# Stores and preparations dealt out differently over the engine queues of a layer-norm, Fourier-mixing and gated-MLP kernel

## The chip, the cores and the metric

The kernel runs on one core of one Trainium2 chip. A core has five engines that take their own instruction streams in order and meet only through semaphores: TensorE (PE; its weight loads are a row of their own, PEld), VectorE (DVE), ScalarE (ACT), GpSimd (POOL) and SyncE (SP). The last two serve here almost only to start transfers. The metric is the device time of one execution in microseconds (us), as the median of several runs; lower is better.

## The reference

```python
xn = _layernorm(x, axis=-1)
a = jnp.einsum("bsd,ed->bse", xn, dft_hid_re)
b = jnp.einsum("bsd,ed->bse", xn, dft_hid_im)
y = jnp.einsum("ts,bse->bte", dft_seq_re, a) - jnp.einsum("ts,bse->bte", dft_seq_im, b)
g = jnp.einsum("bsd,df->bsf", xn, w_gate)
u = jnp.einsum("bsd,df->bsf", xn, w_up)
h = _gelu(g) * u
return x + y + jnp.einsum("bsf,fd->bsd", h, w_down)
```

x is 1 x 2048 x 512, the hidden width of the MLP is 1792, and everything is float32.

## The kernel before

**Products.** A float32 operand is split into a high part (a copy in TensorE's fp32r format) and a low part (the rest). One product is then three matmuls, high x high, high x low and low x high (`mm3`, L86). `split_hi` (L72) is an ACT copy, `split_lo` (L75) a DVE subtraction that needs the ACT copy first. Large products are done by a scheme of seven block products in place of eight (numbers 0 to 6), which needs sums and differences of blocks beforehand, on DVE.

**Stages, in the order of TensorE.** First the layer norm and transposes, with the hidden transform of the first eight row tiles done plainly. Then units 0 to 13: each multiplies one block of gate or up weights with the first half of the rows, applies GELU or the product, and in between runs small down products (`dn`) whose results go to a DRAM buffer `partial` by adding transfers. Then the hidden transform of the second half of the rows, by seven products of four tiles each (`spectral(1, k, i)`, output tiles `sa` and `sb` in PSUM, order `S_ORDER` = 0, 1, 4, 5, 6, 3, 2). Then units 14 to 27 on the second half of the rows. Last, four passes (c, g) = (1,0), (0,0), (1,1), (0,1) of 16 steps each for the sequence transform: a step loads a panel of the two sequence matrices (`pan`, 512 or 768 KB in two transfers), sums its blocks (`sums`, L653 to L656), splits it (`ps` high, `pl` low; the smaller second half in the passes with g = 0 is `ps1`) and adds products into the PSUM banks `m`. The banks of a pass are seeded with the earlier partial sums by ACT (`seed`, L775) and drained at its end.

**What sets the order.** Everything is written out by hand, in program order per engine: an engine executes its instructions in the order of the text, and a wait of one holds all behind it. Preparation for later products is written between the products, so the place in the text decides when DVE and ACT reach it.

**Around the second half's transform.** While product number p runs, `prepare(S_ORDER[p + 2], i)` is called behind each of its four tiles: parts 0 and 2 are the block sums of x and of the weights (`sum_x` L308 to L314, `sum_w` L321 to L329), parts 1 and 3 their splits (`xT4h`, `w1h` and so on). ACT also copies PSUM tiles: `sb<-sa` after product 0 (L243), `a<-sa` after product 1 (L246). All eight PSUM banks are in use, four `sa` and four `sb`, so product 4 gets its first bank when the first `a<-sa` has been copied out. Behind the tiles of the first product stand also the four leftovers of unit 13 (`carry`): `hh`, `hl`, a product with `q`, and a second `hl`.

**Around pass one.** `background(27)` lists the work that the last unit spreads between its own products by cost: sums, split and side tiles (`a`, `s34`) of step 0, then weight splits (`wl<-wd`, `wl<-ws`), then sums and side tiles of step 1. The split of step 1's panel is written behind that, in step 0 (`prepare_step`).

**Around the last passes' ends.** `drain` handles the banks of a pass with g = 1 in the order r = 5, 4, 3, 1, with j = 0, 1: ACT copies bank 5 to `u`, DVE adds bank 4 to give `v` and bank 3 to give the second `u`, which is stored; bank 1 is copied to `o` and stored. `drain_rest` subtracts `v` from four further tiles `x` (L808) and stores them. After the third pass it is called in step 0 of the last pass; after the last pass behind bank 3. All stores but the two halves of the very last tile go through POOL (`store`, L800); those halves, copied by ACT and DVE (L837), go out by the queues of ACT and SP (L838).

Of the kernel before, what the change touches and what calls it, by code (L numbers as in the profile page):

```python
# [24 lines left out]
HD = D // 2  # L25
# [10 lines left out]
def fnet_geglu_kernel(ctx: ExitStack, tc: tile.TileContext, x, xt, cs, dh, wgu, wd, out):  # L36
# [4 lines left out]
    nc = tc.nc  # L41
# [35 lines left out]
    def split(t, src):  # L77
        split_hi(t, src)
        split_lo(t, src)
# [261 lines left out]
                w1[k, j_] = [v[:, j_] for v in w]  # L341
        return w1[k, j], wraw[{0: 0, 1: 1, 3: 3}[k], j] if k in (0, 1, 3) else wsum[k, j]

    def prepare(k, part):
        j = part // 2
        if part % 2 == 0:
            sum_x(k, j)
            sum_w(k, j)
        else:
            split(*x1_split(k, j))  # L350
            split(*w1_split(k, j))

# [104 lines left out]
    items, carry = [], []  # L459
# [18 lines left out]
    def background(n):  # L478
        work = []
        if n == 2 * NP - 1:  # L480
            work = [(None, lambda f=f: advance(f, 0), c) for f, c in ((sum_step, 2), (split_step, 6), (side_split, 3))]

        def put(f, *args, cost=2):
            work.append((None, lambda: f(*args), cost))

        def splits(f, *args, cost=2, then=lambda: None):
            t = []

            def begin():
                t.append(f(*args))  # L490
                split_hi(*t[0])
            work.append((begin, lambda: (split_lo(*t[0]), then()), cost))

        if n % 2 == 0 and n:
            for k in range(4):
                put(h_sum, n // 2 - 1, k)
        if 0 < n < 2 * NP - 1:
            for k in range(4):
                splits(weight_split, n + 1, k, cost=2 if k < 3 else 1)
        if n % 2 == 0 and n:  # L500
            for k in range(4):
                splits(h_split, n // 2 - 1, (2, 1, 0, 3)[k])
        if n % 2 == 0:
            for f in weight_sums(("d", n // 2)):
                put(f, cost=1)
        else:
            for k in range(4) if n < 2 * NP - 1 else (0, 2):
                splits(weight_split, ("d", n // 2), k, cost=2 if k < 3 else 1)
        if n + 2 < 2 * NP:
            for f in weight_sums(n + 2):  # L510
                put(f, cost=1)
        if n in (NP - 2, NP - 1):
            for j in range(2):
                splits(x1_split, n - NP + 2, j)
                splits(w1_split, n - NP + 2, j)
        for k in SIDE_AT.get(n, ()):
            for f in side_sums(k):
                put(f, cost=1)
        if n == 2 * NP - 1:
            put(advance, sum_step, 1)  # L520
            put(advance, side_split, 1, cost=3)
        if 4 <= n < 12:
            t, k = divmod(n - 4, 4)
            put(norm_xr, k // 2, t, k % 2, cost=4)
        return work
# [101 lines left out]
    tokens = {0: list(range(NS)), 1: [0, 1, 2, 3, 4, 12, 5, 13, 6, 14, 7, 15, 8, 9, 10, 11]}  # L627
    steps = [(c, g, n) for c, g in passes for n in tokens[g]]
    pan, pan_hl = {}, {}
    reached = {}  # L630

    def advance(f, upto):
        for k in range(reached.get(f, 0), upto + 1):
            f(k)
        reached[f] = max(upto + 1, reached.get(f, 0))
# [26 lines left out]
    def prepare_step(i):  # L662
        advance(sum_step, i)
        later = sums(i + 1) if reached[sum_step] == i + 1 else []
        reached[sum_step] = max(reached[sum_step], i + 2)
        if reached.get(split_step, 0) <= i < len(steps):
            reached[split_step] = i + 1
            low = [split_begin(i, k) for k in range(2)]
            del pan[i]
            if len(later) < 2:  # L670
                low[0]()
                low.pop(0)
        else:
            low = []
        for k in range(max(len(low), len(later))):
            for f in later[k:k + 1] + low[k:k + 1]:
                f()

    def split_begin(i, k):
        g = steps[i][1]  # L680
        two = g or k == 0
        t = (pair("ps"), pair("pl")) if two else hl_tile("ps1")
        src = pan[i][k]
        split_hi(t, src)
        for h, r in enumerate((((0, 6), (2,)), ((4, 5), (3, 1)))[g][k]):
            pan_hl[i, r] = [v[:, h] for v in t] if two else t
        return lambda: split_lo(t, src)

    def split_step(i):
        if i < len(steps):  # L690
# [106 lines left out]
        nc.gpsimd.dma_start(kept[c, k, j], t)  # L797

    def store(c, h, t, j, src):
        nc.gpsimd.dma_start(out[2 * h + j, 2 * c + t], src)  # L800

    us, vs = {}, {}

    def drain_rest(c):
        for j in range(2):
            for h in range(2):
                t = rest.pop((c, h, j))
                nc.vector.tensor_sub(t, t, vs[j])  # L808
                store(c, h, 1, j, t)

    def drain(c, r, j):
        ps = bank.pop((c, r, j))
        if r in (0, 6):
            t = ship("tot")
            nc.scalar.activation(t, ps, AF.Copy)
            if r == 6:
                keep(c, 0, j, t)
            for u in (5, 1) if r == 0 else (3,):
                nc.gpsimd.dma_start(partial[c, u, j], t, accum_op=OP.add)
        elif r == 2:  # L820
            t = ship("x2")
            nc.vector.tensor_sub(t, rest.pop((c, j)), ps)
            keep(c, 1, j, t)
        elif r == 5:
            us[j] = ship("u")
            nc.scalar.activation(us[j], ps, AF.Copy)
        elif r == 4:
            vs[j] = slot("v")
            nc.vector.tensor_add(vs[j], ps, us[j])
        elif r == 3:  # L830
            nc.vector.tensor_add(us[j], ps, us[j])
            store(c, 1, 0, j, us[j])
        elif (c, j) == (passes[-1][0], 1):
            t = ship("o")
            for (e, f), queue in zip(((nc.scalar.copy, slice(HD)), (nc.vector.tensor_copy, slice(HD, CH))),
                                     (nc.scalar, nc.sync)):
                e(t[:, f], ps[:, f])  # L837
                queue.dma_start(out[j, 2 * c, :, f], t[:, f])  # L838
        else:
            t = ship("o")  # L840
            nc.scalar.activation(t, ps, AF.Copy)
            store(c, 0, 0, j, t)
# [126 lines left out]
        unit(n)  # L969
    xT.clear()  # L970
    xT.update(xT_next)
    for p, k in enumerate(S_ORDER):
        for i in range(TPC):
            spectral(1, k, i)
            if p == 0:
                carry.pop(0)()
            if p + 2 < len(S_ORDER):
                prepare(S_ORDER[p + 2], i)
        xT.update(xT_next)
        if p == 4:  # L980
            load_wd(NP // 2)
# [9 lines left out]
    for i, (c, g, n) in enumerate(steps):  # L991
# [13 lines left out]
        elif at < NS - 1:  # L1005
            for k in range(i + 1, ahead + 1):
                prepare_step(k)
        if at == 0 and p == 3:
            drain_rest(passes[2][0])
        if p == 0:  # L1010
            advance(side_split, at + 2)
            while carry:
# [12 lines left out]
        for r in GROUP[g]:  # L1025
# [9 lines left out]
            if r == 3 and g and at == NS - 1:  # L1035
                if turn:
                    low()
                    del pan[i + 1]
                else:
                    drain_rest(c)  # L1040
            if items and r == 0 and at:
                (items.pop(0)() or (lambda: None))()
        if at == NS - 1:
# [39 lines left out]
```

## Time and profile before

| what | value |
|---|---|
| median of 3 runs | 813.76 us (813.72 to 814.07) |
| the profiled execution's own time | 813.86 us |
| its span, first to last instruction | 812.1 us |
| between the two | 1.8 us |
| DVE, ACT, POOL busy, share of the span | 85%, 62%, 22% |
| transfers | 190.02 MB, mean 234 GB/s |

The page lists busy time by engine; a matmul takes 389 ns from start to end but the next begins while it runs, so what counts on TensorE is the distance between starts. In a row of the timeline the columns are start, duration, engine, line, operation, output and inputs, shapes and count, and in square brackets the idle time of the engine just before and what ended it. In the list of waits they are who waited for whom, then the time in all, the number of times and the longest.

### The profile page before, as it was taken

What the parts mean: (1) busy time and instruction counts of PE and PEld (TensorE: products, weight loads), DVE (VectorE), ACT (ScalarE), POOL (GpSimd) and SP (SyncE); (2) the same over time, 40 slices, a digit from 0 to 9 for tenths busy, and PEclk for the clock granted to TensorE, in tenths of its full rate; (3) what the DMA queues carried; (4) which work ended last, traced back from release to release, by engine and by line L of the source; (5) the groups of instructions that cost most, each with busy time, mean ns of one, the idle gap of its engine ahead of it and who ended that gap; (6) DMA issues with size and microseconds to landing.
All of it is one profiled execution on the core that took longest, in us unless ns stands there. A gap on an engine that the chain in (4) does not pass through costs nothing.

```text
span 812.1 us, 11223 instructions
## 1 busy us (share of the span) xinstructions
PE 800.0 (99%) x3514; PEld 654.3 (81%) x3514; DVE 689.2 (85%) x1210; ACT 500.7 (62%) x880; POOL 178.6 (22%) x271
## 2 busy tenths in 40 slices
PE   8999999999999999999999999999999999999996
PEld 4887887888887888888888878888888888888885
DVE  6778999889899769999889988866898889889982
ACT  5667876675686566676676674755575654365531
POOL 2210212222221322343233230221202411020001
PEclk9999999999999999999999999999999999999999
DMA  9833546967993568988888997998999998589612
GB/s 339 308 105 112 200 118 144 216 123 174 236 234 96 191 141 191 280 265 208 213 192 206 251 272 246 323 345 251 323 396 397 278 404 340 198 279 369 240 52 103
DMA packets 80603, 190.02 MB, mean 234 GB/s; under 512 B 10192, under 2 KB 12768, under 8 KB 80416
## 3 DMA queue, kind: packets, MB, share of 16 engines
q1 hardware_dynamic: 53168, 119.57, 42.7%
q0 software_dynamic: 27088, 69.49, 34.6%
q8 instruction: 27, 0.44, 0.2%
q10 hardware_dynamic: 288, 0.26, 0.1%
q14 instruction: 32, 0.26, 0.1%
HBM read 133.17 MB, written 58.20 MB: 236 GB/s over the span
## 4 chain that ended last, share of the span: by engine, by line
PE 68%; issue 17%; DVE 6%; DMA 3%; ACT 3%; POOL 2%; POOLq 0%; SPq 0%; DVEq 0%; ACTq 0%
PE m L86 18%; PE dn L86 13%; PE b L86 12%; PE a L86 8%; PE c L86 8%; PE xp L86 5%; PE sb L86 2%; DMA qr<-sd 2%; PE sa L86 1%; POOL out_y L800 1%; DMA ar<-ab 1%; DVE ws L370 1%; DVE wl L75 1%; DVE s L431 1%; DVE hl L75 1%
## 5 line engine op out<-in xcount | busy, mean ns | idle before, releaser
L72 ACT ACTIVATE ps<-pan 128x1024 fp32r<-128x1024 f32 x96 | 100.5, 1059 | 93.2 <-PE m L86 48.7
L75 DVE TENSOR_TENSOR pl<-pan,ps 128x1024 fp32r<-128x1024 f32 x96 | 117.8, 1227 | 25.9 <-ACT ps L72 18.3
L456 POOL DMA_DIRECT2D partial<-part x86 | 75.8, 894 | 184.0 <-ACT part L452 172.1
L452 ACT ACTIVATE part<-dn 128x512 f32<-128x512 f32 x106 | 62.5, 601 | 29.5 <-PE dn L86 28.3
L75 DVE TENSOR_TENSOR wl<-ws,wh 128x512 fp32r<-128x512 f32 x84 | 55.3, 686 | 0.0
L86 PE MATMUL m<-ps,bth 128*128 128x512 f32 x128 | 49.8, 389 | 0.0
L86 PE MATMUL m<-pl,bth 128*128 128x512 f32 x128 | 49.8, 389 | 0.0
L86 PE MATMUL m<-ps,btl 128*128 128x512 f32 x128 | 49.8, 389 | 0.0
L72 ACT ACTIVATE wh<-ws 128x512 fp32r<-128x512 f32 x84 | 49.7, 628 | 0.0
L86 PE MATMUL m<-ps,a 128*128 128x512 f32 x128 | 44.7, 390 | 0.0
L593 ACT ACTIVATE w<-b 128x512 f32<-128x512 f32 x28 | 16.7, 597 | 39.1 <-PE b L86 39.0
L596 DVE TENSOR_TENSOR w<-c,w 128x512 f32<-128x512 f32 x28 | 19.4, 691 | 24.8 <-ACT w L593 24.6
L86 PE MATMUL b<-xT3h,w 128*128 128x512 f32 x112 | 39.1, 390 | 0.0
L75 DVE TENSOR_TENSOR htl<-s,hth 128x512 fp32r<-128x512 f32 x56 | 36.0, 689 | 2.9 <-ACT hth L72 2.9
L431 DVE TENSOR_TENSOR s<-s 128x512 f32<-128x512 f32 x56 | 37.4, 688 | 0.9
L86 PE MATMUL m<-ps,qrh 128*128 128x512 f32 x96 | 37.3, 389 | 0.0
L86 PE MATMUL m<-pl,qrh 128*128 128x512 f32 x96 | 37.3, 389 | 0.0
L86 PE MATMUL m<-ps,qrl 128*128 128x512 f32 x96 | 37.3, 389 | 0.0
L72 ACT ACTIVATE hh<-s 128x512 fp32r<-128x512 f32 x42 | 26.5, 635 | 10.7 <-PE dn L86 4.1
L72 ACT ACTIVATE hth<-s 128x512 fp32r<-128x512 f32 x56 | 32.4, 640 | 0.6 <-PE dn L86 0.6
L86 PE MATMUL dn<-hth,wh 128*128 128x512 f32 x80 | 31.1, 389 | 0.0
L86 PE MATMUL dn<-hth,wl 128*128 128x512 f32 x80 | 31.1, 389 | 0.0
(329 smaller groups left out, 2452.3 us busy)
## 6 DMA issues: line engine op xcount, KB each, us to landing
pan<-in_cs SPq DMA_DIRECT2D x96, 512.0 KB, 6.6
partial<-part POOLq DMA_DIRECT2D x106, 256.0 KB, 4.9
wx<-in_wgu SPq DMA_DIRECT2D x56, 256.0 KB, 4.4
abr<-ab SPq DMA_DIRECT2D x32, 256.0 KB, 6.5
pan<-in_cs SPq DMA_DIRECT2D x32, 256.0 KB, 6.5
wd<-in_wd SPq DMA_DIRECT2D x28, 256.0 KB, 4.4
old<-partial POOLq DMA_DIRECT2D x28, 256.0 KB, 6.4
b<-ab SPq DMA_DIRECT2D x20, 256.0 KB, 6.6
```

What stands on the lines that cost most here:

```text
L72: nc.scalar.activation(t[0], src, AF.Copy)
L75: nc.vector.tensor_sub(t[1], src, t[0].bitcast(F32))
L86: nc.tensor.matmul(ps, a[u][:, sl], b[v], start=first and r == 0, stop=last and r == 2, skip_group_check=resumed)
L370: nc.vector.tensor_tensor(r[k][:, h], u, v, op=op)
L431: nc.vector.tensor_sub(t, u, v)
L452: nc.scalar.activation(t, ps[j], AF.Copy)
L456: nc.gpsimd.dma_start(partial[sp, r, j], t, accum_op=OP.add)
L593: nc.scalar.activation(w, b, AF.Copy)
L596: nc.vector.tensor_add(w, c, w)
L800: nc.gpsimd.dma_start(out[2 * h + j, 2 * c + t], src)
```

## The change

Four things move; no arithmetic is added or removed, except that the last tile's two halves get a buffer each.

1. In the second half's transform, `prepare(k)` returns five pieces (sums of half 0; split of x half 0 and sums of half 1; split of the weights half 0; split of x half 1; split of the weights half 1). They go into a list `behind`, one is taken behind each tile, and two behind the first tile of every product but the first. The leftovers of unit 13 move from the first product's four tiles to the second tile of products 5, 6, 3 and 2.
2. In `background(27)` the sums of step 1 come directly behind the side tiles of step 0, and a new piece `begin_early(1, 0)` splits the first part of step 1's panel within the unit, ahead of step 1's side tiles.
3. The four subtractions and stores left from the third pass run two by two in steps 1 and 2 of the last pass in place of four in step 0. In the last pass two of them follow each `v`.
4. Stores of the last pass are issued by SyncE in place of POOL.

```diff
-    def prepare(k, part):
-        j = part // 2
-        if part % 2 == 0:
+    def prepare(k):
+
+        def sums(j):
             sum_x(k, j)
             sum_w(k, j)
-        else:
-            split(*x1_split(k, j))
-            split(*w1_split(k, j))
+
+        return (lambda: sums(0),
+                lambda: (split(*x1_split(k, 0)), sums(1)),
+                lambda: split(*w1_split(k, 0)),
+                lambda: split(*x1_split(k, 1)),
+                lambda: split(*w1_split(k, 1)))
...
-            work = [(None, lambda f=f: advance(f, 0), c) for f, c in ((sum_step, 2), (split_step, 6), (side_split, 3))]
+            work = [(None, lambda f=f, k=k: advance(f, k), c)
+                    for f, k, c in ((sum_step, 0, 2), (split_step, 0, 6), (side_split, 0, 3), (sum_step, 1, 2))]
...
-            put(advance, sum_step, 1)
+            put(begin_early, 1, 0, cost=1)
             put(advance, side_split, 1, cost=3)
...
-            low = [split_begin(i, k) for k in range(2)]
+            low = [early.pop((i, k), None) or split_begin(i, k) for k in range(2)]
...
+    def begin_early(i, k):
+        split_begin(i, k)()
+        early[i, k] = lambda: None
...
-        nc.gpsimd.dma_start(out[2 * h + j, 2 * c + t], src)
+        (nc.sync if c == passes[-1][0] else nc.gpsimd).dma_start(out[2 * h + j, 2 * c + t], src)
...
-    def drain_rest(c):
-        for j in range(2):
-            for h in range(2):
-                t = rest.pop((c, h, j))
-                nc.vector.tensor_sub(t, t, vs[j])
-                store(c, h, 1, j, t)
+    def drain_rest(c, j):
+        for h in range(2):
+            t = rest.pop((c, h, j))
+            nc.vector.tensor_sub(t, t, vs[j])
+            store(c, h, 1, j, t)
...
             nc.vector.tensor_add(vs[j], ps, us[j])
+            if c == passes[-1][0]:
+                drain_rest(c, j)
...
-            t = ship("o")
...
-                e(t[:, f], ps[:, f])
-                queue.dma_start(out[j, 2 * c, :, f], t[:, f])
+                t = ship("o")
+                e(t[:, :HD], ps[:, f])
+                queue.dma_start(out[j, 2 * c, :, f], t[:, :HD])
...
+    behind = []
     for p, k in enumerate(S_ORDER):
+        if p + 2 < len(S_ORDER):
+            behind.extend(prepare(S_ORDER[p + 2]))
         for i in range(TPC):
             spectral(1, k, i)
-            if p == 0:
+            if p > 2 and i == 1 and carry:
                 carry.pop(0)()
-            if p + 2 < len(S_ORDER):
-                prepare(S_ORDER[p + 2], i)
+            for f in behind[:2 if p and i == 0 else 1]:
+                f()
+            del behind[:2 if p and i == 0 else 1]
...
-        if at == 0 and p == 3:
-            drain_rest(passes[2][0])
+        if at in (1, 2) and p == 3:
+            drain_rest(passes[2][0], at - 1)
...
-                else:
-                    drain_rest(c)
```

The order of TensorE's instructions is the same in both programs. **ACT in the second half's transform, first two products, before:**

```order
L243 ACTIVATE sb<-sa 128x512
L72 ACTIVATE hh<-s 128x512
L243 ACTIVATE sb<-sa 128x512
L72 ACTIVATE xT4h<-xraw 128x512
L72 ACTIVATE w1h<-w1s 128x512
L243 ACTIVATE sb<-sa 128x512 x2
L72 ACTIVATE xT4h<-xraw 128x512
L72 ACTIVATE w1h<-w1s 128x512
L246 ACTIVATE a<-sa 128x512 x2
L72 ACTIVATE xT5h<-xraw 128x512
L72 ACTIVATE w1h<-w1s 128x512
L246 ACTIVATE a<-sa 128x512 x2
```

and with the change:

```order
L243 ACTIVATE sb<-sa 128x512 x2
L72 ACTIVATE xT4h<-xraw 128x512
L243 ACTIVATE sb<-sa 128x512
L72 ACTIVATE w1h<-w1s 128x512
L243 ACTIVATE sb<-sa 128x512
L72 ACTIVATE xT4h<-xraw 128x512
L246 ACTIVATE a<-sa 128x512
L72 ACTIVATE w1h<-w1s 128x512
L246 ACTIVATE a<-sa 128x512
L72 ACTIVATE xT5h<-xraw 128x512
L246 ACTIVATE a<-sa 128x512
```

Splits and PSUM copies now alternate, and the leftover `hh` is gone from here. **DVE at the same place, before:**

```order
L308 TENSOR_TENSOR xraw<-xraw 128x512
L321 TENSOR_TENSOR w1s<-d_2678,d_2716 128x512
L75 TENSOR_TENSOR hl<-s,hh 128x512
L75 TENSOR_TENSOR xT4l<-xraw,xT4h 128x512
L75 TENSOR_TENSOR w1l<-w1s,w1h 128x512
L417 SCALAR_TENSOR_TENSOR s<-s,q_2652 128x512
L308 TENSOR_TENSOR xraw<-xraw 128x512
L321 TENSOR_TENSOR w1s<-d_2681,d_2719 128x512
L75 TENSOR_TENSOR hl<-s,hh 128x512
L75 TENSOR_TENSOR xT4l<-xraw,xT4h 128x512
L75 TENSOR_TENSOR w1l<-w1s,w1h 128x512
```

and with the change:

```order
L308 TENSOR_TENSOR xraw<-xraw 128x512
L321 TENSOR_TENSOR w1s<-d_2678,d_2716 128x512
L75 TENSOR_TENSOR xT4l<-xraw,xT4h 128x512
L308 TENSOR_TENSOR xraw<-xraw 128x512
L321 TENSOR_TENSOR w1s<-d_2681,d_2719 128x512
L75 TENSOR_TENSOR w1l<-w1s,w1h 128x512
L75 TENSOR_TENSOR xT4l<-xraw,xT4h 128x512
L75 TENSOR_TENSOR w1l<-w1s,w1h 128x512
```

The second pair of sums stands three instructions earlier (one subtraction of the split and two leftovers are no longer ahead of it). **DVE at the end of unit 27, before pass one, before:**

```order
L417 SCALAR_TENSOR_TENSOR s<-s,w 128x512
L75 TENSOR_TENSOR wl<-wd,wh 128x512
L75 TENSOR_TENSOR wl<-ws,wh 128x512
L419 TENSOR_TENSOR s<-s,b 128x512
L75 TENSOR_TENSOR hl<-s,hh 128x512
L617 TENSOR_TENSOR q_5263<-c,q_5263 128x512
L653 TENSOR_TENSOR pan<-pan,pan_5074 128x512
L75 TENSOR_TENSOR a_5381<-ar,a_5381 128x256
L75 TENSOR_TENSOR s34l<-w_5078,s34h 128x512
L75 TENSOR_TENSOR pl<-pan,ps 128x1024
```

and with the change:

```order
L420 SCALAR_TENSOR_TENSOR s<-s,w 128x512
L657 TENSOR_TENSOR pan<-pan,pan_5074 128x512
L75 TENSOR_TENSOR wl<-wd,wh 128x512
L422 TENSOR_TENSOR s<-s,b 128x512
L75 TENSOR_TENSOR hl<-s,hh 128x512
L621 TENSOR_TENSOR q_5263<-c,q_5263 128x512
L75 TENSOR_TENSOR wl<-ws,wh 128x512
L75 TENSOR_TENSOR pl<-pan,ps 128x1024
L75 TENSOR_TENSOR a_5385<-ar,a_5385 128x256
L75 TENSOR_TENSOR s34l<-w_5078,s34h 128x512
```

Step 1's sum (`pan`) stands five instructions earlier and its low part `pl` two earlier, ahead of the side tiles. On ACT the high part `ps` changes places in the same way with `a` and `s34h` of step 1, and `wh<-ws` now stands between the first two and the last two seeds `m<-old`. **DVE at the end of the program, before:**

```order
L829 TENSOR_TENSOR v<-m,u 128x512 x2
L831 TENSOR_TENSOR u<-m,u 128x512 x2
L808 TENSOR_TENSOR x_7950<-x_7950,v 128x512
L808 TENSOR_TENSOR x_7951<-x_7951,v 128x512
L808 TENSOR_TENSOR x_7956<-x_7956,v 128x512
L808 TENSOR_TENSOR x_7957<-x_7957,v 128x512
L837 COPY o<-m 128x256
```

and SP's last stores with the change, which follow DVE's new order (two `x` behind each `v`, then both `u`):

```order
L808 DMA out_y<-x_7950 128x512
L808 DMA out_y<-x_7951 128x512
L808 DMA out_y<-x_7956 128x512
L808 DMA out_y<-x_7957 128x512
L808 DMA out_y<-u 128x512 x2
L808 DMA out_y<-o 128x512
L847 DMA out_y<-o 128x256
```

Before, SP had only the last of these rows, and POOL had the other seven in the order `u` twice, four `x`, `o`.

More of the change, by code (lines that the diff above doesn't have):

```diff
@@ L629, in fnet_geglu_kernel @@
     pan, pan_hl = {}, {}
-    reached = {}
+    reached, early = {}, {}
     def advance(f, upto):
```

## The prediction

> **What bounds the kernel now.** I read the page's busy times first, then every distance between starts of matmuls, then the waits of the weight loads, and last the timeline around the places found.
>
> ```profile
> PE 800.0 (99%) x3514; PEld 654.3 (81%) x3514; DVE 689.2 (85%) x1210; ACT 500.7 (62%) x880; POOL 178.6 (22%) x271
> ```
>
> TensorE sets the time, and the change leaves its instructions and their order as they are. So a gain can come from two sources only: from stalls of TensorE that the busy share hides, and from what follows the last matmul. The first stall, in the second half's transform (TensorE's timeline):
>
> ```profile
> 250.75 0.39 PE L86 MATMUL sa<-w1h,xT1l 128*128 128x512 f32 x1
> 250.98 0.39 PE L86 MATMUL sa<-w1h,xT1h 128*128 128x512 f32 x1
> 251.21 0.39 PE L86 MATMUL sa<-w1l,xT1h 128*128 128x512 f32 x1
> 251.43 0.39 PE L86 MATMUL sa<-w1h,xT1l 128*128 128x512 f32 x1
> 252.42 0.50 PE L86 MATMUL sa<-w1h,xT4h 128*128 128x512 f32 x1 [0.60 <-ACT a L246]
> 252.75 0.39 PE L86 MATMUL sa<-w1l,xT4h 128*128 128x512 f32 x1
> ```
>
> Undisturbed starts lie (251.43 - 250.75) / 3 = 0.227 us apart. The step to 252.42 is 0.99, and the next one 0.33: a stop costs its wait and about 0.11 more. The stage as a whole begins and unit 14 begins with
>
> ```profile
> 240.54 0.39 PE L86 MATMUL sa<-w1h,xT0h 128*128 128x512 f32 x1
> ```
> ```profile
> 280.09 0.39 PE L86 MATMUL a<-xT0h,wh 128*128 128x512 f32 x1
> ```
>
> That is 39.55 us for 7 products x 4 tiles x 6 = 168 matmuls, which at 0.2267 take 38.09: **1.46 us are lost here**. The waits of the weight loads in this stretch name PSUM copies on ACT as releasers, `a` for two stops (below) and `sb` for a third and smaller one, ahead of them:
>
> ```profile
> PEld sa L86 <- ACT a L246: 1.4, 2, 1.0
> ```
>
> The second place is the start of pass one, in step 1:
>
> ```profile
> 484.32 0.40 PE L86 MATMUL m<-ps,a 128*128 128x512 f32 x1
> 485.38 0.50 PE L86 MATMUL m<-pl,a 128*128 128x512 f32 x1 [0.66 <-DVE pl L75]
> ```
>
> The third is step 2 of the last pass:
>
> ```profile
> 728.73 0.39 PE L86 MATMUL m<-ps,qrb 128*128 128x512 f32 x1
> 729.39 0.50 PE L86 MATMUL m<-pl,qrb 128*128 128x512 f32 x1 [0.27 <-DVE pl L75]
> ```
>
> They cost 1.06 - 0.23 + 0.11 = 0.94 and 0.66 - 0.23 + 0.11 = **0.54 us**, and both times TensorE waits for DVE's low part. The last place is the end. Landings there (the list of transfers; the last figure is us from issue to landing), then the late issues (timeline), and the transfer engines (a table by stretches; its last two columns are their busy share and GB/s):
>
> ```profile
> out_y<-u POOLq DMA_DIRECT2D x2, 256.0 KB, 2.3
> out_y<-o POOLq DMA_DIRECT2D x1, 256.0 KB, 3.8
> out_y<-o ACTq DMA_DIRECT2D x1, 128.0 KB, 2.4
> out_y<-o SPq DMA_DIRECT2D x1, 128.0 KB, 3.1
> ```
>
> ```profile
> 806.06 0.35 ACTq L838 DMA_DIRECT2D out_y<-o  x1
> 806.06 0.42 DVE L837 COPY o<-m 128x256 f32<-128x256 f32 x1
> 806.51 0.34 SPq L838 DMA_DIRECT2D out_y<-o  x1
> 807.13 0.54 POOL L800 DMA_DIRECT2D out_y<-o  x1
> ```
> ```profile
> 805.00:810.50 5.50, 0.62 (x3) 0.19 (x1) 1.46 (x3) 0.37 (x1) 2.36 (x5) 0.96 0.92 334
> ```
>
> The last transfer to be issued is not of the last tile: it is the `o` of j = 0, held in POOL's queue behind four `x`. It lands at 807.13 + 3.8 = 810.93, and the end of the span at 812.06 is 1.13 later. The engines are nearly full until 810.5.
>
> **The change, part by part. First, the second half's transform.** The chain behind the late PSUM copies, on ACT:
>
> ```profile
> 247.03 0.63 ACT L72 ACTIVATE xT4h<-xraw 128x512 fp32r<-128x512 f32 x1 [2.43 <-DVE xraw L308]
> ```
> ```profile
> 250.64 0.63 ACT L72 ACTIVATE xT4h<-xraw 128x512 fp32r<-128x512 f32 x1 [1.41 <-DVE xraw L308]
> 251.25 0.63 ACT L72 ACTIVATE w1h<-w1s 128x512 fp32r<-128x512 f32 x1
> 251.78 1.06 ACT L246 ACTIVATE a<-sa 128x512 f32<-128x512 f32 x2
> ```
>
> and the sum that the second of these splits waits for, on DVE:
>
> ```profile
> 249.92 0.69 DVE L308 TENSOR_TENSOR xraw<-xraw 128x512 f32<-128x512 f32 x1
> ```
>
> ACT stands idle with `xT4h` at the head of its queue, waiting for a sum on DVE, while two PSUM copies whose products are done stand behind it. DVE starts an instruction of this size every 0.60 us (727.51 to 728.12 in the rows of the third part). Three instructions leave the way of the second sum, so it starts at about 248.3 in place of 249.92 (three times 0.60, less some 0.2 in which DVE now waits for the first `xT4h`, done at 247.66). ACT's second `xT4h` then starts near 249.05, and the first `a<-sa` stands directly behind it: 249.05 + 0.53 (ACT's distance, 251.25 to 251.78) = 249.6, landing by 250.2. TensorE wants that bank at 251.4 less what it gained before. Margin: over 1 us. The `sb` copies come at 247.6 and 248.6 by the same count, before TensorE's 248.7 and 250.1. The third `a` waits behind `xT5h`, whose sum follows four more DVE instructions: near 252.6, wanted at 254.1. So all three stops go. The leftovers return behind products 5 to 2: one `hl` of them before the last split of product 2. From the first sum (started near 246.3, as it released ACT at 247.03) to that split the new order has 41 DVE instructions, 24.7 us at 0.60 each, so it is done near 271 plus DVE's own waits. TensorE wants it near 274.1: the stage's new end, 278.6, less four tiles of 1.36, plus four matmuls. Some 3 us are left for waits. Value: **-1.4 us**. Bounds: -1.46 if every loss goes, -0.7 if the copies of the third bank or a late split stop it once more.
>
> **Second, pass one.** ACT ahead of the late split, then DVE:
>
> ```profile
> 482.05 0.42 ACT L72 ACTIVATE a<-ar 128x256 fp32r<-128x256 f32 x1
> 482.36 0.63 ACT L72 ACTIVATE s34h<-w 128x512 fp32r<-128x512 f32 x1
> 483.00 1.06 ACT L72 ACTIVATE ps<-pan 128x1024 fp32r<-128x1024 f32 x1
> ```
> ```profile
> 484.10 1.23 DVE L75 TENSOR_TENSOR pl<-pan,ps 128x1024 fp32r<-128x1024 f32 x1 [0.19 <-ACT ps L72]
> ```
>
> DVE's `pl` starts as soon as `ps` is done, so moving the panel's sum forward on DVE is not what pays. `ps` gets rid of `a` and `s34h` ahead of it (482.05 to 483.00, 0.95 us) but takes on `wh<-ws` (0.53), which stood before the seeds and is now between them. It starts 0.42 earlier, and `pl` with it. TensorE resumes at about 484.97 in place of 485.38. The low part of `a`, now behind `pl`, is ready at about 485.26, just when TensorE comes to it at 485.3. The later seeds come 0.5 us later, near 481.6, when TensorE comes to them; a short stop there would only use up some of the wait that follows. Value: **-0.4 us**. Bounds: -0.1 (the side tile late too) and -0.94 (the whole stop).
>
> **Third, the last pass, steps 1 and 2:**
>
> ```profile
> 725.11 2.50 DVE L808 TENSOR_TENSOR x<-x,v 128x512 f32<-128x512 f32 x4
> 727.51 0.69 DVE L654 TENSOR_TENSOR pan<-pan 128x512 f32<-128x512 f32 x1
> 728.12 1.22 DVE L75 TENSOR_TENSOR pl<-pan,ps 128x1024 fp32r<-128x1024 f32 x1
> ```
>
> With the four `x` out of the way, that `pl` runs from 725.7 to 726.95, 2 us before TensorE asks at 728.96. Two `x` then stand in each of the next two steps (1.25 us each), where by the same count `pl` for step 3 ends near 732.3, wanted at 734.5. Value: **-0.54 us**, bounds -0.3 and -0.54. This and the first gain shift everything behind them alike, since transfers and splits there wait for TensorE to free buffers.
>
> **Fourth, the end.**
>
> ```profile
> 798.93 0.69 DVE L829 TENSOR_TENSOR v<-m,u 128x512 f32<-128x512 f32 x1 [9.89 <-PE m L86]
> ```
>
> The first `x` can be stored at 798.93 + 0.69 + 0.62 (a quarter of the four `x` above) = 800.25. Today the first store waits for a `u`, which by the order comes behind both `v`. Eight such instructions end by about 803.9. Seven stores of 0.262 MB at 334 GB/s take 0.78 us each: 800.25 + 2.3 (a landing on quiet engines, `u`) + 6 x 0.78 = 807.3. So the engines are drained when the halves come. DVE's copy may still follow ACT's (a separate buffer frees it of one tie; the built program keeps a wait on ACT). So SP issues between 806.1, as ACT does now, and 806.5, as SP does now; I take 806.5. A half lands 2.3 to 3.1 later; I take ACT's 2.4, being the nearest. 806.5 + 2.4 + 1.13 = 810.0 in place of 812.06: **-2.0 us**. Bounds: 806.1 + 2.3 + 1.13 gives -2.5, 806.5 + 3.1 + 1.13 gives -1.3.
>
> Sum: 1.4 + 0.4 + 0.54 + 2.0 = 4.34. The profiled execution took 813.86 with a span of 812.06, so 809.5; the median lies 0.1 under it, so **809.4 us**.
>
> **The rivals.** *The end is bound by the transfer engines, not by a queue.* For it: 334 GB/s and a share of 0.92 up to 810.5. Then SP only saves the difference of the last issues, 807.13 - 806.51 = 0.6, and the time is 813.76 - 2.34 - 0.6 = 810.8. Against it: the first store now stands before both `u`, not behind them. The Trainium skill has this rule ("DMA: Bandwidth & Descriptors", section "Issuing engines are not separate DMA queues"): transfers of all queues run on the same 16 engines, and a second issuing engine saves only the time to issue. By that rule the move to SP alone is worth those 0.6 us; the rest of my 2.0 hangs on DVE's order.
>
> *The transform's stop moves instead of going*: the leftovers and the four subtractions behind product 6 crowd DVE, and its own waits for ACT eat the 3 us and 1.2 more before product 2 is split. That gives back 1.2: 810.6. For it: the wait of 1.41 us above shows that ACT and DVE hold each other up. Against it: before, with two leftovers more, product 2 came without a stop.
>
> *DVE becomes the bound in the last pass.* For it:
>
> ```profile
> 740.00:780.00 40.00, 40.00 (x178) 33.14 (x177) 40.00 (x52) 21.11 (x23) 0.00 (x0) 1.00 0.68 243
> 780.00:800.00 20.00, 20.00 (x90) 16.55 (x89) 9.68 (x12) 5.45 (x6) 0.00 (x0) 1.00 0.00 0
> ```
>
> DVE (third pair) is full for 40 us. If TensorE, earlier by the gains of pass one and of steps 1 and 2, caught up with it, those 0.94 would be lost: 810.3. Against it: DVE is done half way through the next 20 us, so it works ahead.
>
> *Better:* the whole stop of pass one goes and the end takes its far bound: 808.4.
>
> *It doesn't do what it says:* the stops return one instruction on, and a half on SP lands behind seven stores as late as POOL's last does, 806.51 + 3.8 + 1.13 = 811.44, so 0.6 is left: 813.1.
>
> *Slower:* SP's queue stops in the transform. The leftovers now hold their buffers to product 2, and as built the load of `wd` waits for TensorE too.
>
> ```profile
> 256.88 2.89 SPq L400 DMA_DIRECT2D wd<-in_wd  x2
> ```
> ```profile
> 295.93 0.42 DVE L370 TENSOR_TENSOR ws<-wd 128x256 f32<-128x256 f32 x1
> ```
>
> Behind it stand unit 16's weights. It decides from 291.5 on, when a landing of 4.4 us (`wd` in the page's list of issues) misses 295.93; to come out slower it must be held to 296. At 300 the loss is 8.5 and the time 817.9. Against it: the leftovers end near 277.
>
> **How the numbers follow.** Forecast 0.62, better 0.08, end by the transfer engines 0.10, transform 0.08, DVE 0.04, not as it says 0.05, slower 0.03. The forecast's own bounds run from 808.6 (1.46 + 0.6 + 0.54 + 2.5) to 811.0 (-1.3 - 0.1 - 0.3 - 1.1), which also takes in three of the rivals. About 0.2% (1.6 us) is what a measurement can tell from no change: faster 0.92, same 0.05, slower 0.03.
>
> **What would show it.** Right: first matmuls of the transform and of unit 14 are 38.1 to 38.3 us apart; the step at pass one shrinks to about 0.65; no gap near step 2 of the last pass; the last landing comes from SP or ACT, about 3 us after the last matmul, with quiet engines before. Wrong: a new wait on `xT2l` or `w1l`, a step over 0.9 at pass one, or engines busy until 809 or later.

## The result and the profile after

The changed kernel takes **808.98 us** (median of 4 runs, 808.97 to 809.03); the kernel before, run beside it on the same chip, 813.74 (813.48 to 814.07). The ratio is 0.9941, with an interval of 0.9924 to 0.9959. The forecast was 809.4, in a range of 808.6 to 811.0.

The page of the profile after, its first line of busy times, and TensorE's timeline at the start of the second half's transform and of unit 14:

```profile
PE 800.0 (99%) x3514; PEld 654.6 (81%) x3514; DVE 688.8 (85%) x1210; ACT 499.5 (62%) x880; POOL 175.4 (22%) x264
```
```profile
240.75 0.39 PE L86 MATMUL sa<-w1h,xT0h 128*128 128x512 f32 x1
```
```profile
278.83 0.39 PE L86 MATMUL a<-xT0h,wh 128*128 128x512 f32 x1
```

TensorE is as busy as before, to the tenth of a microsecond: what shrank is the time in which it stood. The transform takes 278.83 - 240.75 = 38.08 us in place of 39.55, which is what 168 undisturbed matmuls take. In the list of the weight loads' waits after, no row of `sa` is left; of the passes' `m` there are two:

```profile
PEld m L86 <- ACT m L783: 0.7, 2, 0.4
PEld m L86 <- DVE pl L75: 0.5, 1, 0.5
```

Before, the two rows were

```profile
PEld m L86 <- DVE pl L75: 1.8, 2, 1.1
PEld m L86 <- ACT m L775: 0.4, 1, 0.4
```

The wait for `pl` has gone from two times to one: the stop in step 2 of the last pass is gone and the one in pass one is shorter. The wait for ACT's seeds has grown from one to two. TensorE's timeline in pass one shows where:

```profile
480.11 0.39 PE L86 MATMUL m<-ps,a 128*128 128x512 f32 x1
480.41 0.50 PE L86 MATMUL m<-ps,s34h 128*128 128x512 f32 x1
480.74 0.39 PE L86 MATMUL m<-pl,s34h 128*128 128x512 f32 x1
...
483.27 0.39 PE L86 MATMUL m<-ps,a 128*128 128x512 f32 x1
483.68 0.49 PE L86 MATMUL m<-pl,a 128*128 128x512 f32 x1
484.01 0.73 PE L86 MATMUL m<-ps,a 128*128 128x512 f32 x2
484.59 0.39 PE L86 MATMUL m<-pl,a 128*128 128x512 f32 x1
```

The step that was 1.06 is now 483.68 - 483.27 = 0.41. A new, small one has opened ahead of it, 480.11 to 480.41 (0.30, and 0.33 behind it, where 0.23 is undisturbed). It is the seeds of the third product, which come later on ACT. A third break stands behind the step: the two starts from 484.01 on take 0.58, where they took 0.46 before.

The end, by the list of transfers (the last figure is us from issue to landing), the timeline of the last issues, and a table by stretches (last columns: the transfer engines' share and GB/s):

```profile
out_y<-x SPq DMA_DIRECT2D x4, 256.0 KB, 2.1
out_y<-u SPq DMA_DIRECT2D x2, 256.0 KB, 2.3
out_y<-o SPq DMA_DIRECT2D x1, 256.0 KB, 2.1
out_y<-o ACTq DMA_DIRECT2D x1, 128.0 KB, 1.7
out_y<-o SPq DMA_DIRECT2D x1, 128.0 KB, 1.7
```
```profile
802.76 0.33 SPq L808 DMA_DIRECT2D out_y<-o  x1
803.07 0.39 PE L86 MATMUL m<-ps,btl 128*128 128x512 f32 x1
...
803.89 0.35 ACTq L847 DMA_DIRECT2D out_y<-o  x1
803.90 0.42 DVE L846 COPY o<-m 128x256 f32<-128x256 f32 x1 [1.99 <-ACT o L846]
804.35 0.33 SPq L847 DMA_DIRECT2D out_y<-o  x1
```
```profile
801.00:804.50 3.50, 2.45 (x11) 1.69 (x9) 1.34 (x3) 0.97 (x2) 0.00 (x0) 1.00 0.99 370
804.50:804.75 0.25, 0.00 (x0) 0.00 (x0) 0.00 (x0) 0.00 (x0) 0.00 (x0) 1.00 0.02 4
```

The seven stores by SP are through at 804.5, and the transfer engines stand still for a quarter of a microsecond before the two halves reach them. The last half lands at 804.35 + 1.7 = 806.05, 2.98 after the last matmul's start; the end of the span, 807.23, is 1.18 later. DVE's copy of its half still waits for ACT's, as the row in brackets says.

**Where the 4.8 us came from.** Below, e1 to e9 are the experiments of the next section. The table cuts each profiled span at four matmul starts: the transform's first, unit 14's first, pass one's first and the last of all. Every number is a difference between two such rows of one profiled execution, and the last column is the median of its runs (single ones marked).

| kernel | start | transform | units 14-27 | passes | from last start to the end | span | time |
|---|---|---|---|---|---|---|---|
| before | 240.54 | 39.55 | 200.02 | 325.12 | 6.83 | 812.06 | 813.74 |
| after | 240.75 | 38.08 | 200.02 | 324.22 | 4.16 | 807.23 | 808.98 |
| e1, part 1 only | 240.50 | 38.08 | 200.02 | 325.15 | 6.83 | 810.58 | 812.69 |
| e2, leftovers only | 240.58 | 38.33 | 200.02 | 325.14 | 6.83 | 810.90 | 812.67 (one) |
| e3, pieces only | 240.44 | 39.02 | 200.02 | 325.12 | 6.83 | 811.43 | 813.20 (one) |
| e4, part 2 only | 240.92 | 39.49 | 200.03 | 324.80 | 6.83 | 812.06 | 813.83 (one) |
| e5, after, stores by POOL | 240.68 | 38.08 | 200.02 | 324.24 | 4.78 | 807.80 | 809.56 |
| e6, part 4 only | 240.31 | 39.49 | 200.02 | 325.13 | 5.83 | 810.77 | 812.76 |
| e7, after, a split moved | 241.00 | 38.08 | 200.02 | 323.70 | 4.16 | 806.97 | 808.37 |
| e8, after without part 3 | 241.08 | 38.08 | 200.02 | 324.80 | 4.17 | 808.15 | 809.84 |
| e9, e7 with the seeds moved | 240.91 | 38.08 | 199.92 | 323.82 | 4.17 | 806.90 | 808.63 |

After against before: transform -1.47, passes -0.90, end -2.67, and 0.21 lost in the start, which no part of the change touches.

### The profile page after: what moved, and what is told of

Read it like the earlier page. It is cut to its first block, busy times and chain, and to the rows that moved or that the text cites. A ratio compares the mean times of both kernels' runs of the same rounds, so it can differ in the third digit from the quotient of the medians.

```text
span 807.2 us, 11226 instructions
## 1 busy us (share of the span) xinstructions
PE 800.0 (99%) x3514; PEld 654.6 (81%) x3514; DVE 688.8 (85%) x1210; ACT 499.5 (62%) x880; POOL 175.4 (22%) x264
## 4 chain that ended last, share of the span: by engine, by line
PE 95%; DVE 3%; ACT 1%; issue 0%; DVEq 0%
PE m L86 39%; PE dn L86 15%; PE b L86 13%; PE a L86 9%; PE c L86 9%; PE xp L86 5%; PE sa L86 3%; PE sb L86 2%; PE warm L870 1%; PE pt L157 0%; DVE wl L75 0%; DVE wpl L75 0%; DVE ws L373 0%; DVE s L434 0%; ACT hth L72 0%
## 5 line engine op out<-in xcount | busy, mean ns | idle before, releaser
L75 DVE TENSOR_TENSOR pl<-pan,ps 128x1024 fp32r<-128x1024 f32 x96 | 117.5, 1224 | 26.7 <-ACT ps L72 19.0
L75 DVE TENSOR_TENSOR wl<-ws,wh 128x512 fp32r<-128x512 f32 x84 | 55.2, 685 | 0.0
L86 PE MATMUL m<-ps,bth 128*128 128x512 f32 x128 | 49.8, 389 | 0.0
L86 PE MATMUL m<-pl,bth 128*128 128x512 f32 x128 | 49.8, 389 | 0.0
L86 PE MATMUL m<-ps,btl 128*128 128x512 f32 x128 | 49.8, 389 | 0.0
L86 PE MATMUL m<-ps,a 128*128 128x512 f32 x128 | 44.9, 391 | 0.0
L86 PE MATMUL b<-xT3h,w 128*128 128x512 f32 x112 | 39.1, 390 | 0.0
L75 DVE TENSOR_TENSOR htl<-s,hth 128x512 fp32r<-128x512 f32 x56 | 36.0, 687 | 2.9 <-ACT hth L72 2.9
L86 PE MATMUL m<-ps,qrh 128*128 128x512 f32 x96 | 37.3, 389 | 0.0
L86 PE MATMUL m<-pl,qrh 128*128 128x512 f32 x96 | 37.3, 389 | 0.0
L86 PE MATMUL m<-ps,qrl 128*128 128x512 f32 x96 | 37.3, 389 | 0.0
L86 PE MATMUL dn<-htl,wh 128*128 128x512 f32 x80 | 31.1, 389 | 0.0
L86 PE MATMUL dn<-hth,wh 128*128 128x512 f32 x80 | 31.1, 389 | 0.0
```

The costliest lines, as they stand in the source:

```text
L75: nc.vector.tensor_sub(t[1], src, t[0].bitcast(F32))
L86: nc.tensor.matmul(ps, a[u][:, sl], b[v], start=first and r == 0, stop=last and r == 2, skip_group_check=resumed)
```

## The experiments

The theory: the transform's stops come from the leftovers standing on DVE ahead of the second sum, with ACT waiting for that sum; pass one's from `ps` standing behind side tiles on ACT; the end from the order in which DVE makes stores ready, with SP adding little. The rivals: the stops go through the interleaving of pieces, the stops move, and the end is set by the transfer engines or by the issuing queue.

**e1: part 1 of the change alone.** The edit is the new `prepare` and its loop, as the diff of the change shows them.

```diff
-    def prepare(k, part):
+    def prepare(k):
...
-            if p == 0:
+            if p > 2 and i == 1 and carry:
                 carry.pop(0)()
-            if p + 2 < len(S_ORDER):
-                prepare(S_ORDER[p + 2], i)
+            for f in behind[:2 if p and i == 0 else 1]:
+                f()
```

> The kernel before with the first part of the change alone (pieces dealt anew and leftovers moved). My theory: the three stops in the second half's transform go and nothing else changes, so from the first sa matmul to the first a matmul of unit 14 it takes 38.1 us in place of 39.55, and the time falls by 1.4 to 1.5 to about 812.3. Rival (gain is given back later, since units 14 to 27 or the passes are held by another engine): the stage is 38.1 but the time stays at 813.7.

812.69 us (8 runs, 812.38 to 813.17) beside 813.94, ratio 0.9987 (0.9975 to 0.9998). The transform is 38.08 long, without a stop, and everything behind keeps its length: the gain of 1.47 arrives at the end of the span as 812.06 - 810.58 = 1.48. Nothing behind gives it back. (The medians are 1.25 apart; single times of either kernel lie up to 0.8 apart.)

**e2 and e3: the two halves of part 1.** e2 moves only the leftovers, e3 only deals the preparation out in pieces.

```diff
# e2
-            if p == 0:
+            if p > 2 and i == 1 and carry:
                 carry.pop(0)()
# e3
+            for f in behind[:2 if p and i == 0 else 1]:
+                f()
```

> The kernel before with only the leftovers of unit 13 moved behind products 5, 6, 3 and 2; prepare keeps its four old parts. My theory (the sums on DVE are late because of what stands ahead of them): counted on from the rows, the second sum comes 1.2 us earlier and only the small stop for the sb copy stays, 0.2 us, so the stage takes 38.3 us. Rival (the order of splits and PSUM copies on ACT alone makes the stops): the stage stays near 39.5.

> The kernel before with only the pieces of prepare dealt anew; the leftovers stay behind the first product. My theory: PSUM copies come in time, but DVE still does the leftovers first, so the second half of the weights of product 4 is late on DVE: one stop of about 0.8 to 0.9 us in product 4 that waits for w1l instead of a, stage near 39.0. Rival (ACT order alone): no stop, 38.1.

e2: 38.33, as expected, and of the three stops only the smallest, on `sb`, is left (TensorE's timeline):

```profile
248.52 0.39 PE L86 MATMUL sa<-w1h,xT1l 128*128 128x512 f32 x1
248.84 0.50 PE L86 MATMUL sa<-w1h,xT1h 128*128 128x512 f32 x1
```

e3: 39.02, also as expected, and a stop stands one instruction further on than before, for a low part on DVE:

```profile
252.00 0.39 PE L86 MATMUL sa<-w1h,xT4h 128*128 128x512 f32 x1
252.97 0.50 PE L86 MATMUL sa<-w1l,xT4h 128*128 128x512 f32 x1 [0.58 <-DVE w1l L75]
```

So moving the leftovers is worth 39.55 - 38.33 = 1.22 of the 1.47, the pieces alone 0.53, and the last 0.25 need both. With the pieces alone the PSUM copies are in time, and DVE, still with the leftovers in its queue, is late with the next thing that it owes, `w1l`. That is the rival "the stop moves"; it holds for this half of the edit, not for the whole.

**e4: part 2 alone.**

```diff
-            put(advance, sum_step, 1)
+            put(begin_early, 1, 0, cost=1)
...
-            low = [split_begin(i, k) for k in range(2)]
+            low = [early.pop((i, k), None) or split_begin(i, k) for k in range(2)]
```

> The kernel before with only the second part of the change (step 1's sum and first split brought into unit 27). My theory: the step of TensorE at the start of step 1 shrinks from 1.06 to 0.4 to 0.65 us, a small new stop of 0.1 to 0.2 appears at the first s34h matmul of step 0 because the later two seeds come 0.5 later, net gain 0.3 to 0.4 us. Rival (DVE's earlier sum is what pays, the whole stop goes): step of 0.23 and 0.9 gained.

The passes are 0.32 shorter, as expected, with the same breaks as in the kernel after, among them:

```profile
481.70 0.39 PE L86 MATMUL m<-ps,a 128*128 128x512 f32 x1
482.00 0.50 PE L86 MATMUL m<-ps,s34h 128*128 128x512 f32 x1
...
484.85 0.39 PE L86 MATMUL m<-ps,a 128*128 128x512 f32 x1
485.27 0.50 PE L86 MATMUL m<-pl,a 128*128 128x512 f32 x1
```

The time of its one run, 813.83, shows nothing of it: the transform's start came 0.38 later than that of the profiled execution of before. A gain of a third of a microsecond is read from the stage, not from one span.

**e8: the kernel after with part 3 undone**, four subtractions in step 0 of the last pass.

```diff
-        if at in (1, 2) and p == 3:
-            drain_rest(passes[2][0], at - 1)
+        if at == 0 and p == 3:
+            for j in range(2):
+                drain_rest(passes[2][0], j)
```

> The changed kernel with the third part undone: the four subtractions left from the third pass stand in step 0 of the last pass again. My theory: the step of 0.66 us at the start of the last pass's step 2 and the 0.11 behind it return, and the time is the changed kernel's plus 0.5, 809.5. Rival (the stop was a landing of a panel and went by chance of timing): 809.0.

809.84 us (4 runs, 809.74 to 810.03), ratio 0.995 (0.9931 to 0.997), and the passes are 324.80 - 324.22 = 0.58 longer. The time is 0.86 longer; in the profiled execution a start that comes 0.33 later accounts for the rest. The stop is back with its old length and its old waiter:

```profile
727.49 0.39 PE L86 MATMUL m<-ps,qrb 128*128 128x512 f32 x1
728.14 0.50 PE L86 MATMUL m<-pl,qrb 128*128 128x512 f32 x1 [0.27 <-DVE pl L75]
```

**e5 and e6: the end taken apart.** e5 is the kernel after with POOL issuing the stores again; e6 the kernel before with SP issuing them.

```diff
# e5, against after
-        (nc.sync if c == passes[-1][0] else nc.gpsimd).dma_start(out[2 * h + j, 2 * c + t], src)
+        nc.gpsimd.dma_start(out[2 * h + j, 2 * c + t], src)
# e6, against before
-        nc.gpsimd.dma_start(out[2 * h + j, 2 * c + t], src)
+        (nc.sync if c == passes[-1][0] else nc.gpsimd).dma_start(out[2 * h + j, 2 * c + t], src)
```

> The changed kernel with the stores of the last pass issued by POOL again; DVE's new order (two x behind each v) stays. Theory A (the order of DVE makes the gain at the end): the last POOL issue is near 802.75 in place of 807.1 and lands before the two halves, so the time is the changed kernel's plus 0 to 0.7, 809.0 to 809.7. Theory B (the issuing engine makes it): most of the 2.7 us at the end comes back, 811 or more.

> The kernel before with only the stores of the last pass issued by SP; DVE does both v, both u and then the four x as before. Theory A (order): the transfers still begin late, the engines are busy until the last landing, near 809.1 to 809.5 us, and 1.3 to 1.7 us are gained, because one transfer takes 0.68 us by SP as in the changed kernel against 0.78 by POOL. Rule of saved issue time alone: the last issue moves from 807.1 to about 806.9, gain 0.2 to 0.6. Theory B: 2.5 us or more.

e5: 809.56 us (3 runs, 809.31 to 809.57), ratio 0.9947 (0.9925 to 0.997). e6: 812.76 (8 runs, 812.48 to 812.96), ratio 0.9987 (0.9976 to 0.9998). From the last matmul's start to the end: 6.83 before, 5.83 with SP alone, 4.78 with the order alone, 4.16 with both. Landings and late stretches of e5:

```profile
out_y<-x POOLq DMA_DIRECT2D x4, 256.0 KB, 2.4
out_y<-o POOLq DMA_DIRECT2D x1, 256.0 KB, 3.0
out_y<-o SPq DMA_DIRECT2D x1, 128.0 KB, 2.4
```
```profile
803.09 0.54 POOL L808 DMA_DIRECT2D out_y<-o  x1 [0.23 <-issue]
```
```profile
804.30 0.34 SPq L847 DMA_DIRECT2D out_y<-o  x1
```
```profile
801.00:806.00 5.00, 2.41 (x11) 1.67 (x9) 1.28 (x3) 0.97 (x2) 2.18 (x5) 1.00 0.85 311
```

and of e6:

```profile
out_y<-o SPq DMA_DIRECT2D x1, 256.0 KB, 3.1
out_y<-o SPq DMA_DIRECT2D x1, 128.0 KB, 2.9
```
```profile
806.20 0.41 SPq L800 DMA_DIRECT2D out_y<-o  x1
806.71 0.82 SPq L838 DMA_DIRECT2D out_y<-o  x1
```
```profile
805.00:809.00 4.00, 0.34 (x2) 0.00 (x0) 1.18 (x3) 0.37 (x1) 0.00 (x0) 1.00 1.00 372
```

In e5 the last half is issued by SP when it is in the kernel after (804.30 and 804.35, the last matmul starting at 803.02 and 803.07), but it needs 2.4 us and not 1.7: POOL's last store, issued at 803.09, needs 3.0 and is still under way. DVE's order is worth 6.83 - 4.78 = 2.05, the issuing engine 4.78 - 4.16 = 0.62 on top of it, and 1.00 without it; both together 2.67, less than the sum of 3.05. The separate buffers of the last tile's halves moved nothing: before and in e5 the halves are issued 0.83 and 1.28 behind the last matmul's start. The 0.62 of e5 lies in theory A's range. For e6 none of the three readings was right: 1.00 is more than the issue time alone (0.2 to 0.6) and less than theory A (1.3 to 1.7).

Two things differ between the issuing engines. First, the stores begin sooner by SP. The first `u`, before and in e6:

```profile
802.68 0.54 POOL L800 DMA_DIRECT2D out_y<-u  x1 [68.16 <-DVE u L831]
```
```profile
802.01 1.70 SPq L800 DMA_DIRECT2D out_y<-u  x2
```

Counted from the last matmul's start, that is 802.68 - 805.23 = -2.55 and 802.01 - 804.95 = -2.94, 0.39 sooner; the `o` of j = 0 is issued 0.65 sooner (at 1.90 and 1.25), and with DVE's new order 0.38 sooner (0.07 in e5, -0.31 in the kernel after). Second, the transfer engines are fuller by SP. The stretch of e5 above still holds 0.55 us in which the next store has hardly begun to move; from 801.55 to 806.00 the share is 0.92 at 335 GB/s. The stretch of the kernel after that begins with the same store, 800.95 to 804.45, has 0.99 at 374. Without DVE's new order the long busy stretch has 0.95 at 343 before (805.10 to 810.45) and 0.99 at 369 in e6 (804.20 to 809.15).

This splits the 1.00 of e6: the busy stretch begins 0.62 sooner (0.75 ahead of the last matmul's start in place of 0.13) and is 5.35 - 4.95 = 0.40 shorter. With DVE's new order it begins 0.65 sooner (2.12 ahead in place of 1.47), which alone is as much as the end gained, 0.62; since the engines then stand still before the halves come, the two parts can't be told apart there. The Trainium skill ("DMA: Bandwidth & Descriptors", section "Issuing engines are not separate DMA queues") has it that transfers run on the same 16 transfer engines whichever engine started them, so that starting them on several engines only saves the time to start them. The sooner beginning agrees with that: 0.39 of it is the earlier issue, and POOL's issue lasts 0.54 where SP's lasts 0.34. The 0.40 goes beyond it: in the kernel before POOL issues a store every 0.62 us there, and each needs 2.6 to 3.8 to land, so the engines always had stores to move. Why the engines are less full by POOL these runs do not say. The list of queues counts 80 packets for each of POOL's stores and 144 for each of SP's; no run tests whether that matters.

**e7: a better place for one split.** In pass one the split of `ws` stands on ACT between the first and the later seeds. e7 puts it behind the preparation of steps 0 and 1 in the list of unit 27.

```diff
-            for k in range(4) if n < 2 * NP - 1 else (0, 2):
+            for k in range(4) if n < 2 * NP - 1 else (0,):
...
             put(advance, side_split, 1, cost=3)
+            splits(weight_split, ("d", n // 2), 2, cost=1)
```

In the kernel after, ACT's timeline there, and DVE's `pl` behind it:

```profile
478.19 1.13 ACT L783 ACTIVATE m<-old 128x512 f32<-128x512 f32 x2
479.23 0.64 ACT L72 ACTIVATE wh<-ws 128x512 fp32r<-128x512 f32 x1
479.75 1.13 ACT L783 ACTIVATE m<-old 128x512 f32<-128x512 f32 x2
480.79 0.63 ACT L72 ACTIVATE hh<-s 128x512 fp32r<-128x512 f32 x1
481.31 1.06 ACT L72 ACTIVATE ps<-pan 128x1024 fp32r<-128x1024 f32 x1
```
```profile
482.40 1.23 DVE L75 TENSOR_TENSOR pl<-pan,ps 128x1024 fp32r<-128x1024 f32 x1 [0.69 <-ACT ps L72]
```

> The changed kernel with one more thing moved: in unit 27 the weight split wh<-ws, wl<-ws is listed behind step 1's early split and side tiles. My theory: of what is left at pass one, the stop at the first s34h matmul (0.07 + 0.11) and the one in step 1 (0.19 + 0.11 + 0.11) come from that ACT instruction of 0.5 us, so both go and 0.55 to 0.6 us are gained: about 808.4. Rival (the seeds or the panel's transfer hold it): nothing changes, 809.0.

808.37 us (3 runs, 808.29 to 808.75), ratio 0.9935 (0.9912 to 0.9957): the passes are 324.22 - 323.70 = 0.52 shorter than after's, the break at the third product has gone, and of the one in step 1 a step of 0.31 is left. Its median is the lowest of all, but the interval of its ratio overlaps that of the kernel after (0.9924 to 0.9959), so it is the stage that shows the gain.

**e9: the seeds as well.** e9 is e7 with the four seeds one conversion earlier on ACT.

```diff
+        if n == 2 * NP - 1:
+            seed(passes[0][0], GROUP[0][0])
         high(n, (0, 0))
...
-        if n == 2 * NP - 1:
-            seed(passes[0][0], GROUP[0][0])
```

> The kernel with the splits of ws moved behind the first preparation of pass one (the run before, 808.37), and the four seeds of the first step moved one conversion earlier on ScalarE, ahead of wh's first split in unit 27. There a break of about 0.1 remains at the first product of pass one (478.78 to 479.10, a pace of 0.23 us, so about 0.1 too much). Theory A, that break is the wait for the first seed, which begins at 478.44 behind a conversion of 0.63: one conversion (0.52) earlier it is gone, about 0.1 us less, near 808.25, with the end, the transform and the third product as they were. Theory B, the break belongs to the change of the bank's use or to pl, and the seeds are not what is late: nothing moves there, 808.4; and the conversion moved behind the seeds comes two microseconds later, so that if its reader needs it in time a new stop opens in the first step, worth up to 0.5, 808.9.

808.63 us (4 runs, 808.44 to 808.87), ratio 0.9934 (0.9918 to 0.9951): not to be told from e7. (Theory A had it near 808.25.) The break at the first product is gone, as theory A says (no row of `m` waits for ACT any more), but TensorE now arrives earlier at step 1, and stops there for `pl`:

```profile
482.99 0.39 PE L86 MATMUL m<-ps,a 128*128 128x512 f32 x1
483.33 0.49 PE L86 MATMUL m<-pl,a 128*128 128x512 f32 x1
483.67 0.72 PE L86 MATMUL m<-ps,a 128*128 128x512 f32 x2
```

Theory A was right on the wait and wrong on the gain: from unit 14 to the last matmul e7 takes 200.02 + 323.70 = 523.72, e9 199.92 + 323.82 = 523.74.

## Why the prediction was right, and where its sizes were off

**The transform: right.** -1.47 for -1.4; 38.08 apart, where 38.1 to 38.3 was to show it. The chain that it rests on, leftovers on DVE ahead of a sum that ACT waits for, is shown by e2 and e3, and e1 shows that nothing behind takes the gain back. The rival that this stop moves (810.6) fell for the whole edit. The slower rival, SP's queue held by the load of `wd`, has no trace: units 14 to 27 take 200.02 in both kernels.

**Pass one: right, with the foreseen stop.** -0.32 was measured for -0.4, in e4 alone and again as the passes' 0.90 less e8's 0.58. In the kernel after `ps` starts 481.31 - 478.85 = 2.46 behind the pass's first matmul in place of 2.89, which is 0.43 sooner where 0.42 was predicted, and TensorE goes on at 4.83 in place of 5.27. The step shrank to 0.41, further than the 0.65 expected, because the later seeds, half a microsecond later, stop TensorE for (0.30 - 0.23) + (0.33 - 0.23) = 0.17 ahead of it. The prediction named this place and said that such a stop only uses up some of the wait that follows; so it was. What it took too lightly is the low part of `a`, ready "just when TensorE comes to it": behind the step 0.58 - 0.46 = 0.12 is lost again, and 0.44 - 0.12 is the 0.32. In e4 and e9 the list of waits names it (`PEld m L86 <- DVE a L75: 0.2, 1, 0.2`); in the kernel after no row does. e7 shows that the place of the one conversion between the seeds cost 0.52: moved away, it takes the stop at the seeds and nearly all of the step with it.

**The last pass: right.** -0.54 was predicted; undoing it costs 0.58 (e8).

**The end: right mechanism, one mis-sized term.** -2.67 where -2.0 was predicted, and outside its bounds (-1.3 to -2.5). The issue of the last half was right: 806.5 was 1.27 behind the last matmul's start at 805.23, and it came 804.35 - 803.07 = 1.28 behind. From landing to end it was 1.13, and is 1.18. What failed is "a half lands 2.3 to 3.1 later; I take ACT's 2.4": it lands in 1.7. The prediction said itself that the engines are drained when the halves come, but the landings that it took for the halves all ran against stores that were still moving. That drain came sooner than predicted, which the sum does not use: the last of the seven stores was to land 807.3 - 805.23 = 2.07 behind the last matmul's start, and it lands at 802.76 + 2.1 = 804.86, 1.79 behind. The rate of 334 GB/s for it came with a share of 0.92, from a stretch of POOL's stores; by SP it is 370. With POOL issuing them the prediction's end comes out almost to the digit: in e5 it is 1.28 + 2.4 + 1.1 = 4.78, and the sum of the prediction's terms is 1.27 + 2.4 + 1.13 = 4.80. That is no support for it, since it was made for SP.

**The range.** Its ends are not the sum of the parts' own bounds. Those give 1.46 + 0.94 + 0.54 + 2.5 = 5.44 and 0.7 + 0.1 + 0.3 + 1.3 = 2.4, so 808.3 to 811.4; the range was added up with 0.6 for pass one's 0.94 at the near end and to 2.8 in place of 2.4 at the far one. The measured 808.98 lies in both.

**The rivals at the end.** That the transfer engines set the end (810.8) fell: they stand still before the halves come. In DVE's old order they do set it: in e6 they are busy without a break until 809.15. That the change does not do what it says (813.1) fell with it. DVE as the bound of the last pass (810.3) fell too: e4's 0.32 and e8's 0.58 add up to the 0.90 by which the passes shortened.

**The sum.** Predicted 1.4 + 0.4 + 0.54 + 2.0 = 4.34, measured 1.47 + 0.32 + 0.58 + 2.67 - 0.21 = 4.83 of the span (812.06 - 807.23). The error of the forecast time, 0.4 us, is in the main the landing of one half, 0.7, less the 0.21 by which the transform happened to start later.

## What to carry to other kernels

When an engine that never stops for long waits at one place, read the queue of the engine that it waits for, and then the queue of the one behind that: here ACT stood idle for a sum on DVE, and the remedy was to take three unrelated instructions out of DVE's way. At the end of a program count from the first store that can go, not from the last: what moved the end most was the order in which the tiles became ready, and the engine that started the stores sooner and kept the transfer engines fuller came second; a last small store landed quickly (1.7 us) only where the big ones were through (2.4 to 3.1 where they were not). A landing time taken from a busy stretch was too long for a quiet one.

## What the runs showed of the hardware that was not expected

**SP's stores begin sooner than POOL's and keep the transfer engines fuller.** For the second `u` SP issues 0.03 us after DVE is done with it (e6), POOL 0.40 after (before); from the issue of the first store to its first movement it is about 0.8 us by SP and 1.1 by POOL, in both orders. In the same order of work 256 KB landed in 2.1 to 2.3 us by SP and in 2.4 to 3.0 by POOL, with shares of 0.99 and 0.92 (after and e5). Per busy share the rates are nearly the same: 335 / 0.92 = 364 and 374 / 0.99 = 378 GB/s.

**The start varies.** The transform's first matmul comes between 240.31 and 241.08 in these profiled executions, though the work ahead of it is the same. Part of the difference is there from the first microseconds: the twelve warm-up matmuls take 4.49 us in e6, which has the earliest start, and 5.30 in e8, which has the latest.

```profile
1.20 4.49 PE L861 MATMUL warm<-warm 128*128 128x512 bf16 x12 [1.20 <-DVE eps L859]
```
```profile
1.20 5.30 PE L870 MATMUL warm<-warm 128*128 128x512 bf16 x12 [1.20 <-DVE eps L868]
```

Their weight loads start 0.43 us apart to the end in e8; in e6 the last three stand within 0.60 us, so the pace doubles there. The granted clock in the profile's stretches reads 1.00 for both and does not show it. The Trainium skill ("TensorE: Matmul & The Clock Gate", section "Part 1: The HAM clock gate (the "warmup" mystery)") says that the clock rises at the end of a window that runs free of the kernel, so that the number of slow matmuls differs from run to run; the pace in these rows agrees. It is not the whole of the difference: the kernel before has the shortest warm-up, 4.36 us, and starts its transform at 240.54, later than e6. The 0.77 us between the earliest and the latest start are what a gain read from a single span can be wrong by here.
